# First block of a fused attention and MoE kernel: attention by pairs of units, an earlier bias, a constant added on GpSimd, and weights converted two tiles at a time

## The chip, the cores and the metric

The kernel runs on one core of a Trainium2 chip. The metric is the device time of one execution in microseconds. The profile is one execution of its own, whose trace has the start and length of each instruction. PE is TensorE, DVE is VectorE, ACT is ScalarE, POOL is GpSimd and SP is SyncE, which here only issues transfers (DMAs). L335 means line 335 of the kernel before.

## The reference

Attention for 4 batches, 8 heads, 576 positions and 64 channels, with a bias from a small network of the relative position, then two feed-forward stages on 2304 tokens of 512 channels:

```python
scores = scale * np.matmul(q, k.transpose(0, 1, 3, 2))
x = (psi_rel / psi_i)[..., None]
h = np.maximum(x @ w1 + b1, 0.0)
bias = h @ w2
scores = scores + bias.transpose(2, 0, 1)[None, :, :, :]
scores = scores - np.max(scores, axis=-1, keepdims=True)
attn = np.exp(scores)
attn = attn / (np.sum(attn, axis=-1, keepdims=True) + 1e-09)
x = np.matmul(attn, v)             # to 2304 tokens x 512
gate = 1.0 / (1.0 + np.exp(-(x @ w_gate)))
x = gate * (x @ w_val) @ w_out     # 512 -> 1536 -> 512
h = x @ w_in                       # 512 -> 2048
g = h * np.clip(h + 3.0, 0.0, 6.0) / 6.0
out = g @ moe2_w_out               # 2048 -> 512
```

## The kernel before

The queries are cut into five chunks (`QC`: four of 128, one of 64). A unit is one chunk, one pair of heads and one batch: 16 units in a chunk of 128 queries. For a unit TensorE makes the scores (`att_qk`, L335), VectorE subtracts them from the bias and takes the minimum (`att_min`, L350), ScalarE takes the exponential and the sum of each row (`att_exp`, L360), `att_norm` adds 1e-9 to the sums (L367), takes the reciprocal (L368) and scales (L373 on VectorE, or L371 on ScalarE in chunk 1). Then TensorE transposes nine blocks of 128 (`att_tr`, three at a time, L386), ScalarE copies each three out (L389), and TensorE multiplies with the values (`att_av`, L430); `att_x` writes the result as a high and a low half (L455, L456). Multiplies of full float32 are counted double in the trace (x20 for the ten of `att_av`), since each runs as two.

In the lead, only attention of chunk 0 runs, with the bias tables of the first chunks; its order on PE, ACT, DVE and SP is that of the code. Then come five blocks, one for each chunk. A block has 68 steps (`moe_steps`), and a step is 12 products of 128 by 512 (`product`, L613) of a chunk's tokens with one tile of weights; in the last block, with half the columns, steps are shorter and some have eight (L607). Block k also carries the attention of chunk k+1 and the bias of later chunks as events, each with a time in steps; an event is run in the code before the step at or after its time. In block 0 PE and SP keep the order of the code, and a scheduler orders ACT and DVE; in the later blocks only PE keeps it. From chunk 2 on, attention is by pairs of units (`pair_qk`, `pair_soft`, `pair_av`).

Weights come as packed 64-bit words (`wpack`). In block 0 each tile of 512 words is turned into a high and a low half (`w_split`: ACT L575, DVE L576, L577, L580, ACT L585, DVE L586) and stored to `wsp` in DRAM (`w_store`, L591). Later blocks load it from there (`w_load`, L535, 512 KB), `WA` steps ahead of its use. PSUM has two double banks for scores (`s_ps`) and four single banks (`mm_ps`).

## Time and profile before

| | us |
|---|---|
| median of 3 runs | 1105.45 |
| lowest and highest of them | 1104.69 and 1105.76 |
| the profiled execution | 1102.25 |
| its span | 1100.2 |
| TensorE busy in it | 1088.0 |
| VectorE busy in it | 679.8 |

The span is the time from the first to the last instruction in the trace; the execution's own time has some 2 us around it. All starts and windows below are counted from the start of the span. A row with "idle before" names in brackets how long the engine stood still before the instruction and what ended it.

### The profile page before, as it was taken

The page shows a single profiled execution, that of the slowest core. Times are in us where ns is not written, and L with a number is a line of the kernel's source. Part 1 is how long each engine was busy: PE and PEld are TensorE (multiplying, and loading weights), DVE is VectorE, ACT ScalarE, POOL GpSimd, SP SyncE. Part 2 cuts the span into 40 slices and gives each one's busy share as a digit, 9 for nine tenths or more (in the row PEclk, how much of TensorE's full clock was granted, in tenths as well). Part 3 has the DMA queues.
Part 4 walks back from the last instruction along what each step waited for, and adds up shares of the span by engine and source line. Part 5 has one row for each costly group of instructions (what it writes and reads, how often), then busy time and mean ns, then how long its engine had stood idle before and what let it go on. Part 6 is the DMA issues. An engine that isn't in the chain of part 4 may idle for free.

```text
span 1100.2 us, 19627 instructions
## 1 busy us (share of the span) xinstructions
PE 1088.0 (99%) x6964; PEld 873.7 (79%) x6964; DVE 679.8 (62%) x1571; ACT 534.7 (49%) x1087; POOL 129.9 (12%) x248
## 2 busy tenths in 40 slices
PE   8999999999999999999999999999999999999998
PEld 4777777777777787878778878788878888888898
DVE  8899998898972466887735654656352417153433
ACT  7887686798872534555424342444032214123332
...
GB/s 235 369 179 296 376 396 374 387 322 370 392 291 235 212 278 288 283 318 287 308 320 249 288 248 276 263 264 248 287 289 212 286 225 280 212 242 309 370 371 272
DMA packets 118768, 321.96 MB, mean 293 GB/s; under 512 B 21008, under 2 KB 29712, under 8 KB 118672
## 3 DMA queue, kind: packets, MB, share of 16 engines
...
q14 instruction: 40, 0.33, 0.1%
...
## 4 chain that ended last, share of the span: by engine, by line
PE 82%; DVE 7%; ACT 4%; DMA 3%; issue 2%; SPq 1%; DVEq 0%; ACTq 0%
PE ps L613 61%; PE ps L430 7%; PE ps L607 6%; PE ps L477 2%; PE ps L386 2%; PE ps L335 2%; PE ps L171 1%; DVE cm L577 1%; DMA kt<-kd 1%; DVE wp L586 1%; DVE cm L580 1%; PE ps L483 1%; ACT cm L575 1%; DVE s L350 1%; DMA wd<-wpack 1%
## 5 line engine op out<-in xcount | busy, mean ns | idle before, releaser
L613 PE MATMUL ps<-xyh,wp 128*128 128x512 f32 (+1 forms) x1472 | 431.2, 379 | 0.2
L613 PEld LDWEIGHTS ps<-xyh,wp 128*128 128x128 f32 x1472 | 263.3, 188 | 58.1 <-DVE m L499 2.7
L613 PE MATMUL ps<-gh,wp 128*128 128x512 f32 (+1 forms) x980 | 298.9, 385 | 0.4 <-ACT gh L628 0.4
L613 PE MATMUL ps<-xyl,wp 128*128 128x512 f32 x640 | 249.7, 390 | 0.3 <-DVE xyl L632 0.3
L613 PEld LDWEIGHTS ps<-gh,wp 128*128 128x128 f32 x980 | 178.7, 188 | 37.7 <-issue 2.5
L613 PE MATMUL ps<-gl,wp 128*128 128x512 f32 x448 | 174.8, 390 | 0.2 <-DVE gl L630 0.2
L409 POOL DMA_DIRECT2D pT<-t x192 | 94.4, 500 | 495.1 <-DMA wp<-wsp 205.1
L628 ACT ACTIVATE gh<-tmp 128x512 fp32r<-128x512 f32 (+1 forms) x140 | 82.1, 587 | 127.5 <-DVE tmp L651 85.1
L613 PEld LDWEIGHTS ps<-xyl,wp 128*128 128x128 f32 x640 | 120.2, 188 | 24.9 <-DVE xyl L632 0.8
L360 ACT ACTIVATE s<-s,m 128x576 f32<-128x576 f32 x144 | 110.4, 769 | 23.8 <-DVE m L499 17.9
L630 DVE TENSOR_TENSOR gl<-tmp,gh 128x512 fp32r<-128x512 f32 x112 | 76.5, 685 | 35.7 <-ACT gh L628 34.8
L613 PEld LDWEIGHTS ps<-gl,wp 128*128 128x128 f32 x448 | 84.2, 188 | 17.1 <-DVE gl L630 0.7
L430 PEld LDWEIGHTS ps<-pT,vt 128*64 128x64 f32 x1600 | 79.3, 137 | 17.0 <-issue 11.6
L430 PE MATMUL ps<-pT,vt 128*64 128x128 f32 (+1 forms) x1600 | 92.1, 266 | 0.5 <-ACT pT L389 0.4
L657 DVE SCALAR_TENSOR_TENSOR tmp<-tmp,ps 128x512 f32<-128x512 f32 (+1 forms) x80 | 50.0, 628 | 55.2 <-ACT tmp L656 53.6
L651 DVE SCALAR_TENSOR_TENSOR tmp<-tmp,ps 128x512 f32<-128x512 f32 x48 | 32.7, 682 | 74.5 <-PE ps L613 73.8
L656 ACT ACTIVATE tmp<-ps 128x512 f32<-128x512 f32 (+1 forms) x80 | 43.9, 548 | 44.3 <-PE ps L613 44.0
L455 ACT ACTIVATE xyh<-ps 128x128 fp32r<-128x128 f32 (+1 forms) x52 | 16.4, 316 | 98.7 <-PE ps L430 98.5
L681 POOL DMA_DIRECT2D outT<-acc x40 | 27.7, 740 | 269.0 <-DVE acc L672 250.3
L399 DVE STREAM_TRANSPOSE t<-s 128x1152 f32<-128x1152 f32 x40 | 54.3, 1369 | 0.4
L373 DVE TENSOR_SCALAR s<-s,r 128x576 f32<-128x576 f32 x112 | 53.2, 517 | 1.4
L456 DVE TENSOR_TENSOR xyl<-ps,xyh 128x128 fp32r<-128x128 f32 (+1 forms) x48 | 16.0, 333 | 58.9 <-ACT xyh L455 58.6
...
## 6 DMA issues: line engine op xcount, KB each, us to landing
wp<-wsp SPq DMA_DIRECT2D x272, 512.0 KB, 5.1
wd<-wpack SPq DMA_DIRECT2D x68, 512.0 KB, 6.4
wsp<-wp SPq DMA_DIRECT2D x68, 512.0 KB, 6.0
...
pT<-t SPq DMA_DIRECT2D x128, 72.0 KB, 4.5
...
```

Source lines behind the costliest of these rows:

```text
L360: nc.scalar.activation(out=s[:, h], in_=s[:, h], func=AF.Exp, scale=-1.0, bias=d["m"][:, h:h + 1], accum_out=r[:, h:h + 1],)
L373: nc.vector.tensor_scalar(out=s[:, h], in0=s[:, h], scalar1=r[:, h:h + 1], scalar2=None, op0=ALU.mult)
L399: nc.vector.transpose(out=tn_q[0][:, :, x], in_=st[u]["s"].rearrange("p h j -> p (h j)").rearrange("p (t q j) -> p q t j", q=4, j=32),)
L409: (nc.sync if p[0][0] < 4 and i > 1 else nc.gpsimd).dma_start(out=pt[32 * q:32 * q + 32, i].rearrange("j u t i -> j (u t i)"), in_=t[32 * ...
L430: nc.tensor.matmul(out=po[64 * h:64 * h + 64, n * a:n * a + n], lhsT=vt[:, v], rhs=pt[:, m * a:m * a + m, k, :], start=(t == 0), stop=(t = ...
L607: nc.tensor.matmul(out=o, lhsT=w[:, c, :], rhs=x, start=(first and c == 0 and w is wh), stop=(last and c == 3 and w is wh),)
L613: nc.tensor.matmul(out=ps[:, 0:nt], lhsT=w[:, c, :], rhs=x[:, 0:nt], start=(first and c == 0 and i == 0), stop=(last and c == 3 and i == 2),)
L628: nc.scalar.activation(out=hi, in_=src, func=AF.Copy, scale=scale)
L630: nc.vector.tensor_tensor(out=lo, in0=src, in1=hi.bitcast(F32), op=ALU.subtract)
L651: nc.vector.scalar_tensor_tensor(out=th, in0=th, scalar=1.0, in1=ps, op0=ALU.add, op1=ALU.mult)
L656: nc.scalar.activation(out=t, in_=ps, func=AF.Relu, bias=3.0)
L657: nc.vector.scalar_tensor_tensor(out=t, in0=t, scalar=6.0, in1=ps, op0=ALU.min, op1=ALU.mult)
```

## The change

Four things are changed.

1. Attention of chunk 1, which runs in block 0, goes by pairs of units. `pair_qk` makes the scores of two units in a row (for this chunk in full float32: first columns 320 to 575 into two single banks, then columns 0 to 319 into two double banks), `pair_soft` does the softmax of each, `att_trs` makes the nine transposes of a unit in a row into two double banks with two copies by ScalarE, and `pair_av` multiplies both units with their values. First scores stand before step 13 (16 in the order of before), the last values behind step 62 (at the block's end before). The bias of chunk 1 stands at steps from 1.0 on, 1.6 apart (2.0 and 2.0).
2. For chunks 0 and 1 the addition of 1e-9 to the sums is done by GpSimd instead of VectorE.
3. `w_split` converts two tiles at a time, every other step, except for tiles 2 and 3. Its scratch comes from the pools of transposed scores and of the bias. Packed tiles are loaded seven steps ahead.
4. Converted tiles lie in pairs (three pairs instead of six tiles), and the later blocks load four steps ahead instead of five; a pair's two loads are issued together when its space is free.

```diff
 SU = S + 31
-WA = 5
+WA = 4
+WR = 7
 WB = 3
...
     z_p = pool("z", 2)
-    w_p = pool("w", 6)
+    w_p = pool("w", 3)
 
...
         s, r = st[u]["s"], st[u]["r"]
-        nc.vector.tensor_scalar(out=r, in0=r, scalar1=1e-9, scalar2=None, op0=ALU.add)
+        q = nc.gpsimd if u[0] < 2 else nc.vector
+        q.tensor_scalar(out=r, in0=r, scalar1=1e-9, scalar2=None, op0=ALU.add)
         nc.vector.reciprocal(out=r, in_=r)
...
         )
+
+    def att_trs(u):
+
+        d = st[u]
+        pt = d["pt"] = A["pt"].tile([128, 9, NQ], F32, name="pT")
+        p = d["s"].rearrange("p h j -> p (h j)")
+        for k0, nb in ((0, 2), (6, 1)):
+            ps = s_ps()
+            for t in range(3 * nb):
+                nc.tensor.transpose(
+                    out=ps[:, t // 3, t % 3 * NQ:t % 3 * NQ + NQ], in_=p[:, 128 * (k0 + t):128 * (k0 + t) + 128],
+                    identity=id_t,
+                )
+            nc.scalar.activation(
+                out=pt[:, k0:k0 + 3 * nb].rearrange("p (a t) n -> p a (t n)", a=nb),
+                in_=ps[:, 0:nb, 0:3 * NQ], func=AF.Copy,
+            )
 
...
         c, hp, _ = p[0]
-        n = QC[c][1]
+        n, fast = QC[c][1], c in (2, 3)
         tails = [mm_ps(), mm_ps()]
...
                 b = u[2]
-                for i in range(3 if n == NQ else 1):
+                for i in range(3 if fast else 1):
                     for h in range(2):
...
                         o = tails[h][:, w * x:w * x + w] if j0 else st[u]["ps"][:, h, 0:NT]
-                        if n == NQ:
+                        if fast:
                             (qh, ql), (kh, kl) = q_q[c, hp], kv_q[u][0]
...
         att_norm(u)
+        if u[0] == 1:
+            return
         att_turn(p, x)
...
 
-    wq, wf_q = {}, {}
+    wq, wf_q, wp_q = {}, {}, {}
+
+    def w_tiles(n, k=1):
+
+        if n % 2 == 0:
+            wp_q[0] = w_p.tile([128, 2, 2, 512], F32R, name="wp")
+        for x in range(k):
+            wq[n + x] = wp_q[0][:, (n + x) % 2]
+        return wp_q[0][:, n % 2:n % 2 + k]
 
...
         if n < NSTEP:
-            wd = A["wf"].tile([128, 512, 2], U32, name="wd")
-            nc.sync.dma_start(out=wd.rearrange("p a b -> p (a b)"), in_=wpack[n].bitcast(U32))
-            wf_q[n] = wd
+            if n % 2 == 0:
+                wf_q[0] = A["wf"].tile([128, 2, 512, 2], U32, name="wd")
+            nc.sync.dma_start(
+                out=wf_q[0][:, n % 2].rearrange("p a b -> p (a b)"), in_=wpack[n].bitcast(U32)
+            )
+            wf_q[1, n] = wf_q[0][:, n % 2:2]
         else:
-            wp = w_p.tile([128, 2, 4, 128], F32R, name="wp")
-            nc.sync.dma_start(out=wp.rearrange("p s c m -> p s (c m)").bitcast(F32), in_=wsp[n % NSTEP])
-            wq[n] = wp
+            nc.sync.dma_start(out=w_tiles(n)[:, 0].bitcast(F32), in_=wsp[n % NSTEP])
 
...
             nc.sync.dma_start(out=wsp[n], in_=wv.bitcast(F32))
-            del wf_q[n], cm_q[n]
-
-    def w_split(n):
+            del cm_q[n]
+
+    def w_split(n, k=2):
 
...
             return
-        wd = wf_q.pop(n)
-        low, high = wd[:, :, 0], wd[:, :, 1]
-        m = A["cv"].tile([128, 512], U32, name="cm")
-        f = m.bitcast(F32)
+        wd = wf_q[1, n][:, 0:k]
+        low, high = wd[:, :, :, 0], wd[:, :, :, 1]
+        if n < 18:
+            m = A["pt"].tile([128, 9, NQ], F32, name="pT").rearrange("p t n -> p (t n)")
+        else:
+            m = z_p.tile([128, 4, S], F32, name="z").rearrange("p g j -> p (g j)")
+        f = m[:, 0:512 * k].rearrange("p (s a) -> p s a", s=k)
+        m = f.bitcast(U32)
         nc.scalar.activation(out=f, in_=high.bitcast(F32), func=AF.Copy, scale=2.0 ** -112)
...
         )
-        wp = w_p.tile([128, 2, 4, 128], F32R, name="wp")
-        wv = wp.rearrange("p s c m -> p s (c m)")
-        nc.scalar.activation(out=wv[:, 0], in_=f, func=AF.Copy)
-        nc.vector.tensor_tensor(out=wv[:, 1], in0=f, in1=wv[:, 0].bitcast(F32), op=ALU.subtract)
-        wq[n] = wp
+        wv = w_tiles(n, k)
+        nc.scalar.activation(out=wv[:, :, 0], in_=f, func=AF.Copy)
+        nc.vector.tensor_tensor(out=wv[:, :, 1], in0=f, in1=wv[:, :, 0].bitcast(F32), op=ALU.subtract)
 
...
         if 2 <= n < NSTEP:
-            nc.sync.dma_start(out=wsp[n], in_=wq[n].rearrange("p s c m -> p s (c m)").bitcast(F32))
+            nc.sync.dma_start(out=wsp[n], in_=wq[n].bitcast(F32))
 
...
         wp = wq.pop(n)
-        wh, wl = wp[:, 0], wp[:, 1]
+        wh, wl = (wp[:, s].rearrange("p (c m) -> p c m", c=4) for s in range(2))
         if first:
...
     with ExitStack() as lead:
-        for name, bufs in (("pt", 2), ("s", 3), ("k", 6), ("v", 7), ("bo", 3), ("wf", 2), ("cv", 2)):
+        for name, bufs in (("pt", 2), ("s", 3), ("k", 6), ("v", 7), ("bo", 3), ("wf", 1), ("cv", 2)):
             A[name] = lead.enter_context(tc.tile_pool(name=name + "l", bufs=bufs))
...
     conv = ExitStack()
-    for name, bufs in (("pt", 2), ("wf", 4), ("cv", 2)):
+    for name, bufs in (("pt", 2), ("wf", 3)):
         A[name] = conv.enter_context(tc.tile_pool(name=name + "c", bufs=bufs, reuse_waits="tile"))
...
     ctx.enter_context(tc.issue_after(gate_act.ins))
-    for n in range(2, WA + 1):
+    for n in range(2, WR):
         w_load(n)
...
 
-    def chunk_att(c, t0, t1, lag):
+    def chunk_att(c, t0, t1):
 
         us = units[c]
-        d = (t1 - t0) / (len(us) - 1 + lag)
+        ps = [tuple(us[i:i + 2]) for i in range(0, len(us), 2)]
+        d = (t1 - t0 - 6.2) / (len(ps) - 1)
         ev = [
-            (t0 - 2 * d, lambda: att_load(us[0], False)),
-            (t0 - d, lambda: (bias_read(us[0]), load_rows(us[1]), load_k(us[1]))),
+            (t0 - 6, lambda: (load_rows(us[0], False), load_k(us[0]), load_k(us[1]), load_v(us[0]))),
+            (t0 - 1.8, lambda: (bias_read(us[0]), load_v(us[1]))),
         ]
-        for i, u in enumerate(us):
+        for i, p in enumerate(ps):
             a = t0 + d * i
 
-            def first(u=u, nxt=us[i + 2] if i + 2 < len(us) else None):
-                if nxt:
-                    load_rows(nxt)
-                    load_k(nxt)
-                att_qk(u)
-                att_min(u)
-                att_exp(u)
-                att_norm(u)
-            if i:
-                ev.append((a + 0.5, lambda u=u: load_v(u)))
-            for part in range(3):
-                ev.append((a + lag * d - 3 + part, lambda u=u, p=part: att_tr(u, p, mm_ps)))
-            ev.append((a + lag * d - 0.01, lambda u=u: (att_av(u, mm_ps), att_x(u))))
+            def first(p=p, nxt=ps[i + 1] if i + 1 < len(ps) else ()):
+                for u in nxt:
+                    load_rows(u)
+                    load_k(u)
+                pair_qk(p)
+                pair_soft(p, 0)
+
             ev.append((a, first))
+            ev.append((a + 1.5, lambda p=p: pair_soft(p, 1)))
+            if i + 1 < len(ps):
+                ev.append((a + 0.5, lambda p=ps[i + 1]: [load_v(u) for u in p]))
+            for x, u in enumerate(p):
+                ev.append((a + 3.9 + 1.2 * x, lambda u=u: att_trs(u)))
+            ev.append((t1 if i + 1 == len(ps) else a + d - 0.01, lambda p=p: pair_av(p)))
         return ev
...
             ev.append((1.0, lambda: nc.sync.dma_start(out=td_t[:, t0:], in_=td[:, t0:])))
-            ev += chunk_bias(1, 2.0, 2.0, NG1 + 2)
-            ev += chunk_att(1, 15.5, last, 2)
+            ev += chunk_bias(1, 1.0, 1.6, NG1 + 2)
+            ev += chunk_att(1, 12.6, 62.2)
         elif k == 1:
...
             if k == 0:
-                if n + WA + 1 < NSTEP:
-                    w_load(n + WA + 1)
-                for x in range(WB - 1 if i == 0 else WB, WB + 1):
-                    w_store(n + x - 1)
-                    w_split(n + x)
+                if i == 0:
+                    w_split(2, 1)
+                    w_split(3, 1)
+                if n + WR < NSTEP:
+                    w_load(n + WR)
+                w_store(n + 1)
+                if i % 2:
+                    w_split(n + WB)
             if n + WA >= NSTEP:
...
             moe_step(k, i, P, mm_ps)

```

On POOL, from its start to the output of the first block (`biasD` are the bias tables in DRAM, `r` the sums of a unit), there stood:

```order
L977 MEMSET const-uint8-127 128x1
L983 UNCONDITIONAL_BRANCH
L261 DMA biasD_84<-bo 128x2x576 x4
L221 DMA biasD_85<-bo 16x8x607 x8
L681 DMA outT<-acc 256x1x128 x8
```

and now:

```order
L1013 MEMSET const-uint8-127 128x1
L1019 UNCONDITIONAL_BRANCH
L262 DMA biasD_84<-bo 128x2x576 x4
L222 DMA biasD_85<-bo 16x8x607 x4
L369 ISA
L369 TENSOR_SCALAR r<-r 128x2 x16
L222 DMA biasD_85<-bo 16x8x607 x4
L369 TENSOR_SCALAR r<-r 128x2 x16
L713 DMA outT<-acc 256x1x128 x8
```

The 32 additions are new, and so is the ISA row ahead of them, which stands behind the first four stores of the table of chunk 1.

On PE, in the middle of block 0, one unit of before (the order counts a float32 multiply once; between the rows with three transposes stand 12 products):

```order
L613 MATMUL ps<-gh,wp 128x512
L430 MATMUL ps<-pT,vt 64x128 x10
L335 MATMUL ps<-kt,qt 128x288 x4
L386 MATMUL ps<-id_t,s 128x128 x3
L613 MATMUL ps<-gh,wp 128x512
...
L613 MATMUL ps<-gh,wp 128x512
L386 MATMUL ps<-id_t,s 128x128 x3
L613 MATMUL ps<-gh,wp 128x512
```

and one pair of units now (48 products stand behind the scores, 12 between the two rows of transposes and 12 behind them):

```order
L645 MATMUL ps<-xyh,wp 128x512
L449 MATMUL ps<-pT,vt 64x128 x20
L502 MATMUL ps<-kt,qt 128x256 x4
L502 MATMUL ps<-kt,qt 128x320 x4
L645 MATMUL ps<-xyh,wp 128x512
...
L645 MATMUL ps<-xyh,wp 128x512
L404 MATMUL ps<-id_t,s 128x128 x9
L645 MATMUL ps<-xyh,wp 128x512
```

Values and scores of two units stand together, and the transposes are no longer cut into three.

On DVE, at the start of block 0, behind the conversion of tiles 2 and 3 (`cm` before and `pT` now are the scratch, `wd` packed and `wp` converted weights; the first conversion of before is that of tile 4, the second that of tile 5; L651 and L630 belong to the products):

```order
L586 TENSOR_TENSOR wp<-cm,wp 128x512 x2
L576 TENSOR_SCALAR cm<-cm 128x512
L577 SCALAR_TENSOR_TENSOR cm<-wd,cm 128x512
L576 TENSOR_SCALAR cm<-cm 128x512
L580 SCALAR_TENSOR_TENSOR cm<-wd,cm 128x512
L577 SCALAR_TENSOR_TENSOR cm<-wd,cm 128x512
L651 SCALAR_TENSOR_TENSOR tmp<-tmp,ps 128x512
L580 SCALAR_TENSOR_TENSOR cm<-wd,cm 128x512
L586 TENSOR_TENSOR wp<-cm,wp 128x512
L630 TENSOR_TENSOR gl<-tmp,gh 128x512
L586 TENSOR_TENSOR wp<-cm,wp 128x512
```

and now, with tiles 4 and 5 in the first 1024-wide conversion, tiles 6 and 7 in the second:

```order
L619 TENSOR_TENSOR wp<-pT,wp 128x512 x2
L610 TENSOR_SCALAR pT<-pT 128x1024
L611 SCALAR_TENSOR_TENSOR pT<-wd,pT 128x1024
L610 TENSOR_SCALAR pT<-pT 128x1024
L683 SCALAR_TENSOR_TENSOR tmp<-tmp,ps 128x512
L614 SCALAR_TENSOR_TENSOR pT<-wd,pT 128x1024
L611 SCALAR_TENSOR_TENSOR pT<-wd,pT 128x1024
L662 TENSOR_TENSOR gl<-tmp,gh 128x512
L614 SCALAR_TENSOR_TENSOR pT<-wd,pT 128x1024
L619 TENSOR_TENSOR wp<-pT,wp 128x2x512
```

The last row completes tiles 4 and 5 together; before, tile 4 was complete two rows ahead of tile 5.

## Rows read from the trace of the kernel before

**Rows 1.** The page: the span and the engines' busy time.

```profile
span 1100.2 us, 19627 instructions
...
PE 1088.0 (99%) x6964; PEld 873.7 (79%) x6964; DVE 679.8 (62%) x1571; ACT 534.7 (49%) x1087; POOL 129.9 (12%) x248
```

**Rows 2.** What PE waited for: total us, times, longest.

```profile
PE ps L179 <- ACT z L156: 1.2, 3, 0.9
```

**Rows 3.** Stretches: us busy (instructions) of engines, granted clock, DMA share, GB/s.

```profile
200.00:250.00 50.00, 50.00 (x322) 39.16 (x322) 46.92 (x100) 42.71 (x88) 0.00 (x0) 1.00 0.94 343
```

**Rows 4.** Timeline of PE in the lead: start, us, engine, line.

```profile
35.31 1.24 PE L335 MATMUL ps<-kt,qt 64*128 64x288 f32 x8 [0.95 <-DMA kt<-kd]
36.49 1.21 PE L386 MATMUL ps<-id_t,s 128*128 128x128 f32 x9
37.62 1.31 PE L430 MATMUL ps<-pT,vt 128*64 128x128 f32 x20
```

**Rows 5.** Timeline of POOL from the start.

```profile
0.25 0.10 POOL L977 MEMSET const-float32-0.0<- 128x1 f32 x1 [0.25 <-issue]
...
26.46 1.13 POOL L221 DMA_DIRECT2D biasD<-bo  x2 [2.45 <-DVE bo L199]
```

**Rows 6.** Timeline of DVE in the lead.

```profile
28.20 0.17 DVE L368 RECIPROCAL r<-r 128x2 f32<-128x2 f32 x1
```

**Rows 7.** Timeline of PE in block 0, one unit.

```profile
153.43 1.31 PE L430 MATMUL ps<-pT,vt 128*64 128x128 f32 x20
...
156.47 0.39 PE L613 MATMUL ps<-xyl,wp 128*128 128x512 f32 x1
...
158.53 0.39 PE L613 MATMUL ps<-xyl,wp 128*128 128x512 f32 x1
...
159.00 0.49 PE L386 MATMUL ps<-id_t,s 128*128 128x128 f32 x3
159.24 0.47 PE L613 MATMUL ps<-xyh,wp 128*128 128x512 f32 x1
159.56 0.40 PE L613 MATMUL ps<-xyl,wp 128*128 128x512 f32 x1
...
165.27 1.31 PE L430 MATMUL ps<-pT,vt 128*64 128x128 f32 x20
```

**Rows 8.** Timeline of PE in block 1: a pair's values, then a bias.

```profile
470.81 2.40 PE L430 MATMUL ps<-pT,vt 128*64 128x128 f32 x40
473.14 0.96 PE L171 MATMUL ps<-z,w2b_t 128*32 128x448 f32 x8
```

**Rows 9.** Timeline of PE in block 0, the unit with a wait.

```profile
295.43 0.87 PE L430 MATMUL ps<-pT,vt 128*64 128x128 f32 x10
296.68 0.87 PE L430 MATMUL ps<-pT,vt 128*64 128x128 f32 x10 [0.38 <-ACT pT L389]
297.48 1.24 PE L335 MATMUL ps<-kt,qt 64*128 64x288 f32 x8
```

**Rows 10.** Timeline of PE at the end of block 0.

```profile
330.98 0.87 PE L430 MATMUL ps<-pT,vt 128*64 128x128 f32 x10
331.78 0.50 PE L613 MATMUL ps<-xyh,wp 128*128 128x512 f32 x1
```

**Rows 11.** Timeline of DVE at the start of block 0.

```profile
86.34 1.28 DVE L580 SCALAR_TENSOR_TENSOR cm<-wd,cm 128x512 uint32<-128x512 uint32 x2
...
89.30 0.43 DVE L576 TENSOR_SCALAR cm<-cm 128x512 uint32<-128x512 uint32 x1
```

**Rows 12.** Timeline of PE at the start of step 4.

```profile
96.38 0.61 PE L613 MATMUL ps<-xyh,wp 128*128 128x512 f32 x2
```

**Rows 13.** Groups of ACT by shape in block 0: busy us, mean ns.

```profile
L360 ACT ACTIVATE s<-s,m 128x576 f32<-128x576 f32 x16 | 12.3, 771 | 2.0 <-DVE m L350 2.0
```

**Rows 14.** Transfer issues in block 4: KB each, median us to landing.

```profile
wp<-wsp SPq DMA_DIRECT2D x75, 512.0 KB, 5.2
```

**Rows 15.** Timeline of PE in block 4.

```profile
1009.81 3.92 PE L607 MATMUL ps<-xyh,wp 128*128 128x256 f32 x22
```

6 lines of the change are left out of this document (3 added, 3 removed).

## The prediction

> **What bounds the kernel now.** I read the page first: TensorE is busy for 1088.0 of the 1100.2 us [rows 1]. The list of what TensorE waits for comes next, because a nearly full engine can only gain where it still stands still: its longest entry is 1.2 us over three waits, all others are below that [rows 2]. So nothing in this change can win by feeding TensorE sooner, except at single places of less than 1 us. It can win by giving TensorE less to do, and lose by putting a wait on it. The table of stretches gives the reserve of the other engines in the first block: between 200 and 250 us VectorE works 46.92 of 50 us, ScalarE 42.71, and the 16 transfer engines are 94% busy [rows 3]. A wait placed on VectorE there, or a tile converted late, has little room. The granted clock is full in that row, so the clock gives nothing back.
>
> Two stretches then matter. In the lead (attention of the first 128 queries) TensorE's timeline is a row of scores, transposes and values, 1.18, 1.13 and about 1.2 us, with one wait of 0.95 us for a transfer of keys just before 35.31 [rows 4]; from there on it runs through. In the first block each unit (a head pair of one batch) is put between 36 products of 512 columns.
>
> **Attention by pairs.** The period of a unit runs from its values at 153.43 to the next at 165.27, 11.84 us [rows 7]. Products follow each other at (158.53 - 156.47)/9 = 0.229 us [rows 7], so 36 of them are 8.24 and a unit costs 3.60 us, two cost 7.20. Of the new pair, the 40 value multiplies in a row cost 473.14 - 470.81 = 2.33 [rows 8], as measured in the next block; two sets of scores 2 x (36.49 - 35.31) = 2.36 [rows 4] (256 and 320 columns instead of 2 x 288, the same columns); the first product behind a group takes 0.32 instead of 0.229 [rows 7], so 0.09. The nine transposes in a row have no row in a block: three of them between products cost 159.56 - 159.00 - 0.229 = 0.33 [rows 7], which gives 0.99 for nine, and nine in the lead take 1.13 before the next group [rows 4], with 0.09 for the first product 1.22. A pair is therefore 4.78 + 2 x (0.99 to 1.22) = 6.76 to 7.22, and saves 0.44 to nothing. I take the middle, 0.2, since nine in a row are as in the lead and products stand around them as in the block: 8 x 0.2 = **1.6 us gained** (0 to 3.5).
>
> Two single places go with the old order. At 295.43 the values of a unit are split by a wait for the copy of its transposes and last until 297.48, 2.05 us [rows 9] against 1.31 for such a group [rows 4]: **0.7** if no pair meets such a wait (0 otherwise). The last unit's values stand in two halves around the block's end, the first of 331.78 - 330.98 = 0.80 [rows 10]; two halves are 1.60 against 1.31: **0.3**.
>
> ScalarE's share of a pair is the same work: copies of 768 and 384 instead of three of 384, and the same exponentials and scalings. The earlier bias of the second chunk moves the same 32 multiplies one step ahead; TensorE has no wait there, so I cost it at nothing, covered by products.
>
> **The constant on GpSimd.** The add of 1e-9 to a unit's sums leaves VectorE (32 of them). It is worth about 0.2 us of VectorE per unit, as the reciprocal of the same size behind it takes 0.17 [rows 6], and TensorE doesn't wait for VectorE at these places, so the gain is nothing. The price is another. The order of GpSimd shows a new instruction of its own, the row that reads only ISA, ahead of the first add; by its name in the program it reloads the engine's code library. It stands behind the transfer issue that ends at 26.46 + 1.13 = 27.59 [rows 5], and the reciprocal behind it is wanted at 28.20 [rows 6]. VectorE's reciprocal waits for the add, behind it on VectorE the scaling, behind that TensorE's transposes. In this stretch VectorE's chain sets TensorE's pace, and the wait of 0.95 for keys at 35.31 [rows 4] is the reserve that I find behind it; from there TensorE's rows follow each other. So a reload that costs R delays the rest of the program by 27.59 + R + 0.2 - 28.20 - 0.95, that is by R - 1.4 if R is above 1.4, and by nothing below.
>
> No row of before has such an instruction. The nearest on its engine are the first memsets, 0.10 us each [rows 5]; if code has to be fetched, the nearest is a transfer, 5.2 us from issue to landing [rows 14]. The bounds are then 0 and 5.2 - 1.4 = 3.8 us. I take nothing, by the rows of the same engine, which runs these memsets within the first half microsecond of the program, before any code could have been fetched for them. This is a choice between two ends, not a middle, and the other end is a rival below.
>
> The Trainium skill, "GPSIMD Engine Reference", section on how an instruction is dispatched, speaks against my choice: the first call to freshly loaded kernel code pays about 6 us with no visible instruction. By that figure the delay would be an estimated 4.6 us instead of none. No row of before shows such a load.
>
> **Conversion over two tiles.** Each step used to convert one tile of 512 columns with four VectorE instructions and two of ScalarE; now every other step converts two at once, so fewer instructions with the same elements. VectorE's saving is hidden like the above. What it costs is that two tiles come ready together, the first of them later. The only place without reserve is the start. In the order of VectorE behind the two single tiles stand, up to the last instruction of tiles 4 and 5: two shifts, five 1024-wide two-input operations and two 512-wide ones of the products. A 512-wide shift took 0.43 us, a two-input one 1.28/2 = 0.64 [rows 11]; with double width at double price that is 2 x 0.86 + 5 x 1.28 + 2 x 0.64 = 9.4 us. Starting at 89.30 [rows 11] it ends at 98.7, while step 4 starts at 96.38 [rows 12] and asks for the low half in its third product, at about 96.9. That would be a wait of 1.8 us; fixed parts of an instruction are paid once for two tiles, and the first products need not be on time either, so the lower bound is 0. I take **0.5 lost**, nearer to 0, because back-to-back starts on VectorE are closer together than the durations in a row.
>
> **Loads in the later blocks.** Loads are issued in pairs, four steps ahead instead of five, for the even tile. In the last block 22 products of a stage take 3.92 us [rows 15], so a step of eight takes 1.43 and four steps 5.7 us, while a load lands in 5.2 (median) [rows 14]. Steps of the blocks before are nearly twice as long (12 x 0.229 = 2.7). The even tile asks for nothing that the odd one didn't have behind it in the same queue, so I cost it at nothing; above, it is bounded by a few loads that land late in the last block, 2 us.
>
> **Sum.** 1.6 + 0.7 + 0.3 - 0.5 = 2.1 us less. The profiled execution took 1102.25 us, its span 1100.2, so 1100.15 there; the runs' median is 1105.45, 3.2 above the profiled one, and with the same difference the forecast is **1103.3 us**.
>
> **Rivals.** (a) *The reload costs a transfer's time.* 3.8 us lost at 28 us less 2.1 gained: 1.7 slower, 1107.1. For it: an instruction that names a reload has bytes to bring, and TensorE's transposes there are chained to the reciprocal through VectorE. Against it: GpSimd needs nothing of the kind for its first instructions [rows 5]. It decides from R = 3.5 us on, where the loss equals the gain. By the Trainium skill's 6 us ("GPSIMD Engine Reference", the same section) it would come out at an estimated 1108.0.
>
> (b) *A pair's softmax is late.* Between a pair's scores and the first nine transposes stand four steps, 48 x 0.229 = 11.0 us. ScalarE alone needs 4 exponentials of 0.77 [rows 13] and up to 4 scalings of the same size, 6.2 us, and VectorE must first bring eight minima through a queue that now holds 1024-wide instructions of up to 1.28 us (twice the 0.64 above). If each pair waits 0.5 us, eight lose 4.0: 1107.3. Against it: the second unit's transposes stand 12 products behind the first's, and a similar pair form runs in the next blocks, while the longest entry among TensorE's waits is 1.2 us in all [rows 2].
>
> (c) *Nothing but the stalls changes*, nine transposes at the dear end: 0.7 + 0.3 - 0.5 = 0.5 faster, 1104.9; part of my own case.
>
> **Chances.** My case, with (c) as its upper part: 0.50, from 1100.9 (all terms at their good ends: 3.5 + 0.7 + 0.3 gained) to 1105.9 (no saving in the pairs, 1.5 at step 4), half of it more than 0.2% faster. Rival (a) 0.32, from 1105 to 1109. Rival (b) 0.18, from 1104 to 1109. A measurement of this kernel tells about 0.2% (2.2 us) from no change: faster means below 1103.2, slower above 1107.7. My case splits 0.25 and 0.25; (a) 0.02, 0.13 and 0.17; (b) 0.03, 0.04 and 0.11. Sums: faster 0.30, same 0.42, slower 0.28. The range that leaves out one in ten on each side is 1101.0 to 1108.6.
>
> **What would show it.** Right: TensorE's timeline passes the transposes at 36.49 [rows 4] at the same time, pairs in the first block cost about 7.0 us beyond their products, and no wait for a scaled tile. Wrong: a gap of TensorE of over 2 us between 28 and 36, with VectorE waiting for GpSimd's sum (rival a); waits of the new transposes for ScalarE's scaling (rival b); a wait of about 1 us at the fifth step; or waits for loaded tiles in the last block.

## The result, and the profile after

The changed kernel takes 1113.20 us in the median of 4 runs (1112.57 to 1115.27), the kernel before 1105.07 (1104.41 to 1105.76). The ratio is 1.0087, with a 95% interval of 1.0075 to 1.0100: slower by 8.1 us in the medians and by some 9.6 by the ratio, outside the range of 1101.0 to 1108.6 that was forecast. The profiled execution of the changed kernel took 1115.27 us, the highest of the four, at a mean granted clock of 0.993 over its span; in the other three it was 0.995 to 0.997.

The page has TensorE as busy as before [rows 1], and 13 us more of span (8 in the medians). The row of the granted clock has a slice below 9, which the kernel before doesn't have:

```profile
span 1113.5 us, 19187 instructions
...
PE 1089.2 (98%) x6964; PEld 880.2 (79%) x6964; DVE 669.8 (60%) x1467; ACT 522.6 (47%) x999; POOL 141.6 (13%) x280
...
PEclk9999999999989999999999999999999999999999
```

The stretch from 100 to 333 us, most of block 0, of the changed kernel (busy us and instructions of PE, PEld, DVE, ACT and POOL, then granted clock, share of the transfer engines, GB/s), and below it of the kernel before:

```profile
100.00:333.00 233.00, 223.75 (x1316) 179.73 (x1315) 196.19 (x342) 169.62 (x274) 11.99 (x22) 0.97 0.93 344
```

```profile
100.00:333.00 233.00, 232.54 (x1365) 181.10 (x1358) 204.68 (x426) 181.08 (x357) 6.31 (x10) 1.00 0.97 361
```

TensorE stood still for 233.00 - 223.75 = 9.25 us instead of 0.46, and its mean granted clock is 0.97. VectorE, ScalarE and the transfer engines all do less per microsecond than before, so over the whole stretch none of them is busier than the kernel before had it. Measured from the first product of block 0 to the first of block 1 (product 817 in the trace), the block takes 261.6 us instead of 251.8; the lead is 0.3 us shorter, and blocks 1 to 4 together are 3.8 longer.

What TensorE waited for from 80 to 333 us, the four longest entries (us in total, times, longest):

```profile
PE ps L645 <- DVE wp L619: 2.3, 2, 1.8
PE ps L645 <- ACT gh L660: 2.0, 1, 2.0
PE ps L404 <- ACT pT L408: 2.0, 1, 2.0
PE ps L645 <- DVE gl L662: 1.8, 1, 1.8
```

Converted weights (`wp`, L619), the copies of transposes (`pT`, L408), and the high and low halves of a step's result (`gh`, `gl`, L660 and L662): four kinds of work of ScalarE and VectorE, each late once or twice, the longest of each by some 2 us. Before, the list had only one of these, 0.4 us for a copy. The wait of the transposes (L404) for a copy is one for space: the nine transposes of a pair's second unit need the double banks that the copies of the first unit's transposes (L408) empty.

**GpSimd's addition** is the first thing that was in doubt. GpSimd's timeline in the lead, and VectorE's first reciprocal:

```profile
26.30 1.12 POOL L222 DMA_DIRECT2D biasD<-bo  x2 [2.44 <-DVE bo L200]
27.63 0.21 POOL L369 TENSOR_SCALAR r<-r 128x2 f32<-128x2 f32 x1 [0.21 <-ACT s L361]
```

```profile
27.88 0.17 DVE L370 RECIPROCAL r<-r 128x2 f32<-128x2 f32 x1
```

The first addition starts 0.21 us behind the last transfer issue, a time put down to ScalarE's sum that it needs, and takes 0.21. The reload ahead of it shows no time. The reciprocal stands at 27.88 instead of 28.20 [rows 6], and TensorE's transposes of [rows 4] at 36.15 instead of 36.49:

```profile
34.98 1.24 PE L336 MATMUL ps<-kt,qt 64*128 64x288 f32 x8 [0.93 <-DMA kt<-kd]
36.15 1.20 PE L388 MATMUL ps<-id_t,s 128*128 128x128 f32 x9
```

**A pair** has this shape in the timeline of TensorE: values at 173.51, scores at 175.85 and 177.99 the first product, then nine transposes in a row at 189.01:

```profile
173.51 2.40 PE L449 MATMUL ps<-pT,vt 128*64 128x128 f32 x40
175.85 2.21 PE L502 MATMUL ps<-kt,qt 64*128 64x256 f32 x16
177.99 0.50 PE L645 MATMUL ps<-gh,wp 128*128 128x512 f32 x1
178.32 0.39 PE L645 MATMUL ps<-gl,wp 128*128 128x512 f32 x1
...
189.01 1.15 PE L404 MATMUL ps<-id_t,s 128*128 128x128 f32 x9
189.91 0.48 PE L645 MATMUL ps<-gh,wp 128*128 128x512 f32 x1
190.22 0.39 PE L645 MATMUL ps<-gl,wp 128*128 128x512 f32 x1
```

From the values to the second product are 178.32 - 173.51 - 0.229 = 4.58 us, and nine transposes cost 190.22 - 189.01 - 0.229 = 0.98. A pair is 4.58 + 2 x 0.98 = 6.5 us, with the product ahead of it, 0.08 longer than 0.229, some 6.6, against 7.20 for two units [rows 7]: 0.6 saved, some 4.5 us in eight pairs.

**A wait** is dearer than it looks. TensorE at the end of the block:

```profile
316.76 0.39 PE L645 MATMUL ps<-gh,wp 128*128 128x512 f32 x1
319.15 0.50 PE L645 MATMUL ps<-gh,wp 128*128 128x512 f32 x1 [2.01 <-ACT gh L660]
321.47 0.80 PE L645 MATMUL ps<-gl,wp 128*128 128x512 f32 x1 [1.81 <-DVE gl L662]
322.07 1.05 PE L645 MATMUL ps<-gh,wp 128*128 128x512 f32 x2
322.92 0.63 PE L645 MATMUL ps<-gl,wp 128*128 128x512 f32 x1
...
326.55 0.84 PE L645 MATMUL ps<-gh,wp 128*128 128x512 f32 x2
327.22 0.40 PE L645 MATMUL ps<-gl,wp 128*128 128x512 f32 x1
```

```profile
322.07:326.55 4.48, 4.48 (x17) 3.80 (x16) 4.48 (x10) 4.25 (x7) 1.34 (x2) 0.50 0.27 102
```

Two waits of 2.01 and 1.81 us stand behind each other, and then products start 0.43 apart ((322.92 - 322.07) / 2) instead of 0.229, up to 326.55. The granted clock of that stretch is 0.50 (second row): TensorE is at the lower of its two levels, 1.2 GHz instead of 2.4. A mean granted clock of 0.97 over 233 us is 7 us of full clock not granted (part of it while TensorE stood still), where before had none. Not every wait is followed by such a stretch: in pairs_only (below) TensorE stood still for 6.4 us, at most 1.55 at a time, and in single_converted once for 1.77, both at a mean clock of 1.00 from 100 to 333 us. ScalarE just ahead of the wait of 2.01 us shows the cause there, with VectorE's row for its operand in front:

```profile
314.57 0.69 DVE L689 SCALAR_TENSOR_TENSOR tmp<-tmp,ps 128x512 f32<-128x512 f32 x1 [0.51 <-ACT tmp L688]
```

```profile
314.95 1.14 ACT L609 ACTIVATE z<-wd 128x1024 f32<-128x1024 f32 x1
315.98 0.59 ACT L688 ACTIVATE tmp<-ps 128x512 f32<-128x512 f32 x1
316.46 1.06 ACT L618 ACTIVATE wp<-z 128x1024 fp32r<-128x1024 f32 x1
317.40 1.18 ACT L408 ACTIVATE pT<-ps 128x768 f32<-128x768 f32 x2
318.46 1.16 ACT L660 ACTIVATE gh<-tmp 128x512 fp32r<-128x512 f32 x2
```

TensorE wants the high half (L660). Its operand (`tmp`, L689) is complete at 315.26, yet it stands at 318.46, behind a scaled copy of two packed tiles (L609, 1.14 us), a high half of two converted tiles (L618, 1.06) and the copies of transposes (L408, 1.18). Long instructions ahead of it in ScalarE's queue held back the short one that was waited for.

### The profile page after: what moved, and what is told of

It is laid out like the page before. It is cut to its first block, busy times and chain, and to the rows that moved or that the text cites. A ratio compares the mean times of both kernels' runs of the same rounds, so it can differ in the third digit from the quotient of the medians.

```text
span 1113.5 us, 19187 instructions
## 1 busy us (share of the span) xinstructions
PE 1089.2 (98%) x6964; PEld 880.2 (79%) x6964; DVE 669.8 (60%) x1467; ACT 522.6 (47%) x999; POOL 141.6 (13%) x280
## 4 chain that ended last, share of the span: by engine, by line
PE 76%; DVE 8%; DMA 7%; ACT 5%; issue 2%; SPq 1%; POOL 0%; DVEq 0%; ACTq 0%
PE ps L645 56%; PE ps L449 6%; PE ps L639 5%; PE ps L496 2%; DMA wp<-wsp 2%; DMA wd<-wpack 2%; DMA kt<-kd 2%; DVE wp L619 1%; PE ps L388 1%; DVE s L518 1%; PE ps L336 1%; ACT s L361 1%; PE ps L502 1%; PE ps L172 1%; ACT s L373 1%
## 5 line engine op out<-in xcount | busy, mean ns | idle before, releaser
L645 PE MATMUL ps<-gh,wp 128*128 128x512 f32 (+1 forms) x980 | 295.9, 384 | 2.9 <-ACT gh L660 2.9
L660 ACT ACTIVATE gh<-tmp 128x512 fp32r<-128x512 f32 (+1 forms) x140 | 82.0, 587 | 132.1 <-DVE tmp L683 86.9
L662 DVE TENSOR_TENSOR gl<-tmp,gh 128x512 fp32r<-128x512 f32 x112 | 76.4, 686 | 36.1 <-ACT gh L660 35.4
L449 PE MATMUL ps<-pT,vt 128*64 128x128 f32 (+1 forms) x1600 | 89.1, 265 | 1.5 <-DMA wp<-wsp 1.4
L689 DVE SCALAR_TENSOR_TENSOR tmp<-tmp,ps 128x512 f32<-128x512 f32 (+1 forms) x80 | 49.9, 628 | 53.2 <-ACT tmp L688 51.8
L474 ACT ACTIVATE xyh<-ps 128x256 fp32r<-128x256 f32 (+1 forms) x44 | 15.1, 344 | 97.7 <-PE ps L449 97.7
L679 ACT ACTIVATE tmp<-ps 128x512 f32<-128x512 f32 x48 | 28.5, 593 | 60.2 <-PE ps L645 60.2
L518 DVE CUSTOM_DVE_ANT_0 s<-ps,bm,m 128x320 f32<-128x320 f32 x112 | 56.2, 545 | 0.0
```

The source lines that it names most:

```text
L449: nc.tensor.matmul(out=po[64 * h:64 * h + 64, n * a:n * a + n], lhsT=vt[:, v], rhs=pt[:, m * a:m * a + m, k, :], start=(t == 0), stop=(t = ...
L518: nc.vector.tensor_tensor_reduce(out=d["s"][:, h, j0:j1], in0=x, in1=bm_q[c, hp][:, h, j0:j1], scale=-(D ** -0.5), scalar=top, op0=ALU.add ...
L645: nc.tensor.matmul(out=ps[:, 0:nt], lhsT=w[:, c, :], rhs=x[:, 0:nt], start=(first and c == 0 and i == 0), stop=(last and c == 3 and i == 2),)
L660: nc.scalar.activation(out=hi, in_=src, func=AF.Copy, scale=scale)
L662: nc.vector.tensor_tensor(out=lo, in0=src, in1=hi.bitcast(F32), op=ALU.subtract)
L689: nc.vector.scalar_tensor_tensor(out=t, in0=t, scalar=6.0, in1=ps, op0=ALU.min, op1=ALU.mult)
```

## The experiments

The list of waits gave the first theory, T: conversion by two tiles makes the waits, as converted tiles and what stands behind 1024-wide instructions come late, while pairs only save. Rival S put them down to the pairs, whose softmax comes in bursts and late; rival C to both together.

The experiments were timed beside runs of the kernel before with medians of 1103.3 to 1103.5 us; the changed kernel's ratio is that of the first result. The table gives for each kernel the ratio to it, the length of block 0 (start of the 817th product less start of the first, from the trace of one profiled execution), and how long TensorE stood still from 100 to 333 us (233 less its busy time there). The last two columns come from one execution each, so a difference of 1 us in them says little by itself (executions of the kernel before differ by 3).

| kernel | ratio, 95% interval | block 0, us | TensorE idle, us |
|---|---|---|---|
| before | | 251.8 | 0.5 |
| changed | 1.0087, 1.0075 to 1.0100 | 261.6 | 9.3 |
| pairs_only | 1.0024, 1.0015 to 1.0034 | 254.5 | 6.4 |
| two_tiles_only | 1.0071, 1.0054 to 1.0087 | 259.9 | 5.1 |
| add_on_vector | 1.0117, 1.0090 to 1.0143 | 260.8 | 10.6 |
| five_ahead | 1.0102, 1.0087 to 1.0117 | 261.6 | 10.0 |
| before_half_loads | 1.0005, 0.9996 to 1.0014 | 253.0 | 1.6 |
| pairs_half_loads | 1.0075, 1.0057 to 1.0093 | 262.8 | 9.1 |
| after_half_loads | 1.0155, 1.0140 to 1.0170 | 267.4 | 13.5 |
| pairs_late | 1.0037, 1.0026 to 1.0048 | 255.7 | 6.6 |
| pairs_light | 0.9964, 0.9950 to 0.9977 | 247.9 | 2.1 |
| after_light | 1.0001, 0.9992 to 1.0011 | 252.1 | 4.3 |
| before_light | 0.9977, 0.9967 to 0.9987 | 249.7 | 0.0 |
| pairs_slack | 1.0029, 1.0017 to 1.0041 | 256.4 | 7.2 |
| single_in_pairs | 1.0072, 1.0045 to 1.0099 | 257.9 | 4.6 |
| single_packed | 1.0047, 1.0032 to 1.0062 | 256.4 | 4.7 |
| single_converted | 1.0022, 1.0013 to 1.0032 | 254.3 | 3.2 |
| pairs_sub_pool | 1.0241, 1.0221 to 1.0261 | 277.9 | 18.7 |
| before_short | 1.0027, 1.0016 to 1.0038 | 250.6 | 0.0 |
| pairs_short | 1.0093, 1.0066 to 1.0119 | 253.0 | 5.2 |

### Which part of the change

**pairs_only**, the kernel before with the pairs (`chunk_att`, `att_trs` and the lines of `pair_qk` and `pair_soft` as in the change, not repeated here) and the earlier bias:

```diff
-            ev += chunk_bias(1, 2.0, 2.0, NG1 + 2)
-            ev += chunk_att(1, 15.5, last, 2)
+            ev += chunk_bias(1, 1.0, 1.6, NG1 + 2)
+            ev += chunk_att(1, 12.6, 62.2)
```

> The kernel before with attention of chunk 1 by pairs and the earlier bias alone: conversion by single tiles, loads five ahead and the constant on VectorE stay. Theory T (the conversion by two tiles with three pair buffers makes the waits of block 0; the pairs themselves are cheaper): no wait of TensorE above 0.5 us between 100 and 330 us, pairs at 6.7 us beyond their products, 1100 to 1102.5 us. Rival S (a pair's softmax bunches work on ScalarE and VectorE and its chain is late): waits of over 1 us in block 0 as in the changed kernel, 1107 or more. Rival C (only both together run short): like T here.

**two_tiles_only**, the changed kernel with those lines, `chunk_att` and `att_norm` as they were:

> The changed kernel with attention of chunk 1 by units and the bias times of before, and the constant on VectorE: conversion by two tiles, three pair buffers and loads four ahead stay. Theory T: waits of TensorE for converted tiles or evictions in block 0, 1109 to 1116 us. Rival S: no such waits, 1104 to 1107 (only the later blocks' waits for loads, about 1 to 2 us). Rival C (only both together run short): 1104 to 1107.

**add_on_vector**:

```diff
-        q = nc.gpsimd if u[0] < 2 else nc.vector
-        q.tensor_scalar(out=r, in0=r, scalar1=1e-9, scalar2=None, op0=ALU.add)
+        nc.vector.tensor_scalar(out=r, in0=r, scalar1=1e-9, scalar2=None, op0=ALU.add)
```

> The changed kernel with the addition of the constant back on VectorE. Theory T and rivals S and C: the same as the changed kernel, 1111.5 to 1115 us, since GpSimd's additions took 0.21 us and no gap stood ahead of the first. Rival G (VectorE's wait for GpSimd, 1.2 us at most in block 0, disturbs the order there): 1 to 4 us faster than the changed kernel.

**five_ahead**:

```diff
-WA = 4
+WA = 5
```

> The changed kernel with loads of the later blocks five steps ahead again, still in three pair buffers. If the shorter lead makes the later blocks' waits for loads (1.4, 0.8 and 0.2 us in the changed kernel's trace, with what follows them): 1.5 to 3 us faster than the changed kernel. If the pair buffers make them (a load can only start when both tiles of a pair are used up): the same as the changed kernel, within 1 us.

Both halves lose, and nearly add up: the pairs 0.24%, conversion by two tiles 0.71%, together 0.87% (1.17% in add_on_vector, where the addition is on VectorE as in the two halves). So theory T held for the conversion alone, and C fell. For the pairs S held in kind, with waits of over 1 us, but 1106.0 us lies between what T and S had said. The pairs save on TensorE and still make the block 2.7 us longer. In pairs_only TensorE waits, among others, for the scalings and copies of their own softmax (waits of TensorE in pairs_only):

```profile
PE ps L402 <- ACT s L371: 2.8, 2, 1.5
PE ps L402 <- ACT pT L406: 1.4, 2, 0.7
```

The addition on VectorE gave nothing back, rather the opposite, so no cost of GpSimd's part shows. Loads five ahead made blocks 1 to 4 shorter by 2.3 us in the profile (766.0 against 768.3 to the end of the span), but the timed ratio shows no gain. In two_tiles_only, with loads four ahead as well, these blocks took 765.0, only 0.5 more than before. So what the lead of the loads costs stays open.

### Transfers

The first block keeps the transfer engines 97% busy in the kernel before (the row above). Theory D held them to be the limit. From tile 5 on, packed words of every other tile (in the changed kernel of every other pair) aren't loaded, and the tile ahead of it is converted again, so the output is another one:

```diff
-        if n < NSTEP:
+        if 4 <= n < NSTEP and n % 2:
+            wf_q[n] = wf_q[n - 1]
+        elif n < NSTEP:
```

> The kernel before, but from tile 5 on every odd tile in block 0 is converted from the packed words of the even tile ahead of it, whose load serves both (wrong weights, the same instructions, 32 loads of 512 KB less of the first block's traffic of 87.6 MB). Theory D (block 0 runs at the limit of the transfer engines, so in the kernel before the loads arrive just in time and TensorE doesn't wait): no change, within 2 us of the kernel before. If the transfers held the kernel before too: 2 us faster or more.

> Attention by pairs and the earlier bias alone, with the same 32 loads left out (wrong weights, the same instructions). Theory D: the waits of TensorE in block 0 (7 us in the run of pairs alone) go for the most part, what the pairs save on TensorE is seen: 3 to 5 us faster than pairs alone, and 1 to 3 us faster than the kernel before. Rival O (the waits come from the order of ScalarE's and VectorE's queues, not from data): within 1.5 us of pairs alone.

> The changed kernel, but from tile 4 on every other pair of tiles in block 0 is converted from the packed words of the pair ahead (wrong weights, the same instructions, 32 loads of 512 KB less). Theory D: the waits in block 0 and the drops of the clock behind them go, 1100 to 1105 us. Rival O (the 1024-wide instructions in the queues of ScalarE and VectorE make the waits whatever the data do): 1110 us or more. Both in part: between.

**pairs_late** starts the pairs and the bias as late as the units had them:

```diff
-            ev += chunk_bias(1, 1.0, 1.6, NG1 + 2)
-            ev += chunk_att(1, 12.6, 62.2)
+            ev += chunk_bias(1, 2.0, 2.0, NG1 + 2)
+            ev += chunk_att(1, 15.5, 66.0)
```

> Attention by pairs alone, with the bias of chunk 1 at its old times (steps 2.0 on, 2.0 apart) and the pairs started at step 15.5 as the units were, ending at 66. Theory D (the early bias and the early loads of chunk 1 put more traffic into the stretch from 100 to 130 us, where the packed words then come late): the first waits (0.35, 1.55 and 0.53 us between 120 and 150 us, and the late products there) go, 2 to 4 us faster than pairs alone, 1101 to 1104 us on the scale of 1103.5 for the kernel before. Rival O: the same as pairs alone, within 1.5 us.

Theory D, as it was put, fell. With a fifth of the traffic gone the pairs got 6 us slower, and the changed kernel 7; no theory had said that. The stretch from 100 to 333 us of pairs_half_loads:

```profile
100.00:333.00 233.00, 223.87 (x1307) 180.93 (x1306) 205.50 (x475) 176.90 (x329) 3.55 (x6) 0.96 0.78 276
```

The transfer engines are at 0.78, and TensorE is idle for 9.1 us. Since the scheduler orders ScalarE and VectorE anew for each kernel, this run has another order there than pairs_only; it shows that the waits come without full transfer engines, not that the loads are free. Packed words still came late in it, later than in pairs_only (longest wait 2.72 us). ScalarE waited 6.40 us for them, and SyncE, whose transfers keep the order of the code, had stood 4.5 us before a load of values (L305) that waited for TensorE, ahead of the load of these words (L552, issued at 228.84; the second row is from SyncE's waits from 205 to 240 us):

```profile
235.25 0.67 ACT L596 ACTIVATE cm<-wd 128x512 f32<-128x512 f32 x1 [6.40 <-DMA wd<-wpack]
```

```profile
SPq L305 <- PE ps L447: 5.2, 2, 4.5
```

So the order of SyncE's transfers is a rival that no run tests. The later start gained nothing either.

### VectorE's time

Of the bit instructions of a conversion, one (L577 of before, which joins the lowest three bits of each weight) is left out, so weights are rounded down in these bits:

```diff
-        nc.vector.scalar_tensor_tensor(
-            out=m, in0=low, scalar=29, in1=m, op0=ALU.logical_shift_right, op1=ALU.bitwise_or
-        )
```

> Attention by pairs alone, with one VectorE instruction per converted tile in block 0 left out (the OR of the lowest three bits of each weight, about 0.6 us of VectorE per step of 2.73 us). Theory U (VectorE and ScalarE have too little time left in block 0, so a pair's burst of minima, exponentials and scalings makes converted tiles and evictions late): the waits in block 0 shrink to under 2 us of 7, 1100 to 1102.5 us. Rival L (a pair's own chain from scores to transposes is too long for its four steps, whatever else the engines do): less than 1.5 us faster than pairs alone.

> The changed kernel with the same VectorE instruction left out per two tiles (about 1.15 us of VectorE in 5.5). Theory U: 5 us or more faster than the changed kernel, 1107 or less. Rival B (three buffers of two tiles, and stores that have to land before a buffer is free, make the waits): within 2 us of the changed kernel.

> The kernel before with the same VectorE instruction of the conversion left out (the lowest three bits of each weight). Theory U (VectorE's time runs short with pairs, and not before, where TensorE hardly waits): within 1 us of the kernel before. If the instruction's time is paid in every kernel: 4 us or more faster.

**pairs_slack** gives a pair's chain one step more:

```diff
-                ev.append((a + 3.9 + 1.2 * x, lambda u=u: att_trs(u)))
+                ev.append((a + 4.9 + 1.1 * x, lambda u=u: att_trs(u)))
```

> Attention by pairs alone, with the transposes of each pair one step later (at 4.9 and 6.0 steps behind the scores instead of 3.9 and 5.1). Rival L: the waits for scalings ahead of the transposes (2.8 us, and 1.4 us for copies) go, 3 us or more faster than pairs alone. Theory U: those waits move to others (evictions, converted tiles), less than 1.5 us faster.

One step more changed nothing in the time, and TensorE's waits for scalings gave way to others (2.1 and 1.4 us for converted tiles, 1.7 for copies): rival L fell. One instruction less per tile changed much. The stretch from 100 to 333 us of pairs_only and of pairs_light:

```profile
100.00:333.00 233.00, 226.60 (x1347) 181.09 (x1346) 209.86 (x483) 179.50 (x336) 5.03 (x8) 1.00 0.96 353
```

```profile
100.00:333.00 233.00, 230.91 (x1374) 187.01 (x1374) 176.93 (x420) 176.62 (x333) 6.31 (x11) 1.00 0.97 366
```

VectorE goes from 209.86 us of 233 (90%) to 176.93 (76%), and TensorE's idle time from 6.4 to 2.1. The pairs are then level with before_light or slightly ahead (0.13%, with overlapping intervals; 247.9 against 249.7 us in block 0) instead of 0.24% behind before. The kernel before gains too, 0.23%, more than theory U had said, though its TensorE hardly waited there. So part of the pairs' 4.5 us is there when VectorE has room. VectorE's share alone doesn't decide, though: in the same stretch it was 88% in the kernel before and 89% in before_short (below), where TensorE stood still for 0.5 and 0.0 us. That bursts of minima, exponentials and scalings make something late is the reading that fits; it isn't shown apart from the new order that each edit brings.

The changed kernel gained most, from 1.0087 to 1.0001, where rival B had allowed 2 us. So what its buffers cost (next section) depends on VectorE's room as well.

### The two-tile conversion

**single_in_pairs** converts each tile by itself, with all buffers as in two_tiles_only:

```diff
-                if i % 2:
-                    w_split(n + WB)
+                if n + WB > 3:
+                    w_split(n + WB, 1)
```

> The kernel with two-tile conversion alone, but each tile converted by itself, one per step, in the same three pair buffers, with the same scratch, the same loads seven steps ahead and four steps ahead in the later blocks. If the 1024-wide instructions (a queue is held twice as long, both tiles are only ready together) make the loss: 1103 to 1106 us, no waits for converted tiles in block 0. Rival B (the buffers and their stores): 1108 us or more, with such waits.

**single_packed** then gives packed tiles six buffers of their own, **single_converted** instead the converted ones (the lines that take the tiles alone; first one kernel's, then the other's):

```diff
-                wf_q[0] = A["wf"].tile([128, 2, 512, 2], U32, name="wd")
+            wd = A["wf"].tile([128, 1, 512, 2], U32, name="wd")
...
-            wp_q[0] = w_p.tile([128, 2, 2, 512], F32R, name="wp")
+        t = w_p.tile([128, 1, 2, 512], F32R, name="wp")
```

> Single tiles converted one per step with three pair buffers for converted tiles as in the run of single tiles in pairs, but with six single buffers for packed tiles, so that a load waits for one conversion only. If the packed pairs made the loss (loads can start only after both tiles are converted): 1103 to 1106 us, no wait over 1 us between 130 and 150 us. If the converted pairs and their stores did: 1108 or more.

> The same with packed tiles still in three pair buffers, and six single buffers for converted tiles, so that a conversion waits for one tile's products and store only. If the converted pairs made the loss: 1103 to 1106 us. If the packed pairs did: 1108 or more, with late packed tiles between 115 and 140 us.

I had held the 1024-wide instructions to be the cost. No such cost shows: single tiles in pair buffers are as slow (1.0072 against 1.0071, each to within 0.2 to 0.3%). Buffers by single tiles give back 0.50% for the converted ones, clear of noise, and 0.25% for the packed ones, where the intervals overlap; at 1108.1 single_packed also met what was expected if the converted pairs made the loss, and single_converted, at 1106.2, nearly did. So most of the loss is in the pairs of buffers for converted tiles: three pairs hold as much as six tiles, but a half that is used up can't be filled before the other half is used up and stored as well. The 0.22% that single_converted still loses isn't divided further: packed pairs, loads seven and four ahead, and the shared scratch are left in it, and no run had both kinds of buffers single. In single_in_pairs the longest wait is at one place: ScalarE waits for packed tiles, and 10 us later TensorE waits 2.37 us for a converted one (the mean granted clock from 130 to 150 us is 0.91).

```profile
129.79 0.67 ACT L608 ACTIVATE z<-wd 128x512 f32<-128x512 f32 x1 [1.66 <-DMA wd<-wpack]
...
132.28 0.68 ACT L608 ACTIVATE z<-wd 128x512 f32<-128x512 f32 x1 [0.26 <-DMA wd<-wpack]
```

```profile
141.00 0.73 PE L644 MATMUL ps<-xyh,wp 128*128 128x512 f32 x2 [2.37 <-DVE wp L618]
```

### Two attempts at a faster version

**pairs_sub_pool** has the last instruction of a conversion on GpSimd:

```diff
-        nc.vector.tensor_tensor(out=wv[:, 1], in0=f, in1=wv[:, 0].bitcast(F32), op=ALU.subtract)
+        nc.gpsimd.tensor_tensor(out=wv[:, 1], in0=f, in1=wv[:, 0].bitcast(F32), op=ALU.subtract)
```

> Attention by pairs alone, with the last instruction of each conversion in block 0 (the subtraction that makes the low half, 0.6 us of VectorE per step) on GpSimd, nothing left out. Theory U: if GpSimd takes no more than some 2 us for one, the waits in block 0 shrink as with the instruction left out, 1099 to 1103 us, faster than the kernel before. If GpSimd takes over 2.7 us for one, it becomes the bound of the conversion: 1120 us or more.

**before_short** and **pairs_short** join lowest bits and sign first, in a scratch `e`, so that only one VectorE instruction stands between ScalarE's two:

```diff
+        nc.vector.tensor_scalar(out=e, in0=low, scalar1=29, scalar2=None, op0=ALU.logical_shift_right)
+        nc.vector.scalar_tensor_tensor(
+            out=e, in0=high, scalar=0x80000000, in1=e, op0=ALU.bitwise_and, op1=ALU.bitwise_or
+        )
+        nc.vector.scalar_tensor_tensor(
+            out=m, in0=m, scalar=3, in1=e, op0=ALU.logical_shift_left, op1=ALU.bitwise_or
+        )
```

> The kernel before with the conversion's three bit instructions in another order, the same result: the lowest bits and the sign are joined first, in a scratch of their own, without ScalarE's scaled copy, and only the third instruction needs that copy. VectorE's time is the same, the chain behind ScalarE is one instruction instead of three (1.2 us shorter). If the chain's length makes the waits: 1 to 3 us faster than the kernel before. If VectorE's time does: within 1 us of it.

> Attention by pairs alone with the same shorter chain. If the chain's length makes the pairs' waits: 3 us or more faster than pairs alone (2.5 above the kernel before), and as fast as the kernel before or faster. If VectorE's time does (theory U): within 1.5 us of pairs alone.

GpSimd takes 1.37 us for one subtraction, within what was expected, and the kernel still lost 2.4%. Groups of VectorE by shape from 150 to 250 us, in pairs_only and in pairs_sub_pool, and GpSimd's in the latter (busy us, mean ns):

```profile
L599 DVE SCALAR_TENSOR_TENSOR cm<-wd,cm 128x512 uint32<-128x512 uint32 x28 | 19.2, 687 | 0.3
L596 DVE SCALAR_TENSOR_TENSOR cm<-wd,cm 128x512 uint32<-128x512 uint32 x27 | 18.6, 688 | 0.4
```

```profile
L599 DVE SCALAR_TENSOR_TENSOR cm<-wd,cm 128x512 uint32<-128x512 uint32 x25 | 23.0, 918 | 0.5
L596 DVE SCALAR_TENSOR_TENSOR cm<-wd,cm 128x512 uint32<-128x512 uint32 x25 | 22.7, 909 | 0.6
```

```profile
L605 POOL TENSOR_TENSOR wp<-cm,wp 128x512 fp32r<-128x512 f32 x25 | 34.3, 1373 | 66.4 <-ACT wp L604 57.2 <-PE ps L500 4.5 <-DMA wsp<-wp 2.6
```

VectorE's two-input bit instructions went from 0.69 to 0.91 us in the mean. This mean hides two kinds, as rows of both engines show:

```profile
198.75 1.29 POOL L605 TENSOR_TENSOR wp<-cm,wp 128x512 fp32r<-128x512 f32 x1 [1.36 <-ACT wp L604]
```

```profile
198.90 1.69 DVE L596 SCALAR_TENSOR_TENSOR cm<-wd,cm 128x512 uint32<-128x512 uint32 x1
200.62 0.69 DVE L599 SCALAR_TENSOR_TENSOR cm<-wd,cm 128x512 uint32<-128x512 uint32 x1
```

The instruction that starts under GpSimd's subtraction (198.75 to 200.04) takes 1.69 us, ending 0.55 behind it; the next, with GpSimd idle, takes its usual 0.69. Of VectorE's 57 rows of L599 from 100 to 333 us, the 38 without such overlap take 0.69 in the mean. So VectorE lost back part of the time that it had given away. VectorE's share of the stretch is 84% here, below that of pairs_only, and TensorE's waits are the most of all (from 80 to 360 us 5.4 for copies, 4.2 for scalings, 3.2 for GpSimd's tiles): theory U's answer failed, and what makes the whole loss isn't shown.

The shorter chain made block 0 a little shorter (250.6 against 251.8, and 253.0 against 254.5 with pairs), so the chain may have a part, of 1 to 1.5 us in one execution each. Timed, both were slower than either answer had said (1106.64 and 1110.83 us, the latter with executions from 1108.16 to 1119.13, of which the lowest was profiled). In the profiles the loss came in the lead, which grew from 83.9 to 89.8 us (88.9 with pairs). VectorE's timeline there, in before_short:

```profile
72.77 0.43 DVE L577 TENSOR_SCALAR ce<-wd 128x512 uint32<-128x512 uint32 x1 [3.10 <-DMA wd<-wpack]
```

The first instruction no longer depends on ScalarE, so the scheduler put one for a tile of block 0 into the lead's queue, where it waited 3.10 us for its load, with the softmax of the lead behind it. Held back to block 0, before_short would be a candidate; this wasn't tried. No version without work left out beat the kernel before.

## Why the prediction was wrong

- *GpSimd's constant at nothing*: right, and so was the choice between the two ends. The first addition ran at 27.63, and TensorE passed the lead 0.3 us sooner. The rule of the Trainium skill ("GPSIMD Engine Reference", section on instruction dispatch), some 6 us for a first call, would have put it at an estimated 33; no run here shows such a time.
- *Pairs, 1.6 us gained*: right in direction, and too small. The work of eight pairs measured some 4.5 less, since nine transposes in a row cost 0.98, the cheap end of 0.99 to 1.22, and values and scores 4.66 instead of 4.78.
- *The two single places, 1.0*: both went, but the new order made others: 2.01 and 1.81 us at the block's end, 2.0 ahead of a pair's transposes.
- *Conversion over two tiles, 0.5 lost at step 4*: the step that failed. The place that it priced was no loss: VectorE completed tiles 4 and 5 at 97.81, and the bias multiplies, moved ahead of step 4 by the change, held its first product back to 97.88 (timelines of the changed kernel):

```profile
96.13 0.39 PE L645 MATMUL ps<-xyh,wp 128*128 128x512 f32 x1
96.45 1.50 PE L172 MATMUL ps<-z,w2b_t 128*32 128x384 f32 x16
97.88 0.50 PE L645 MATMUL ps<-xyh,wp 128*128 128x512 f32 x1
```

```profile
96.59 1.22 DVE L619 TENSOR_TENSOR wp<-pT,wp 128x1024 fp32r<-128x1024 f32 x1
```

  That this place cost nothing was luck of the order: in two_tiles_only, where the bias stands later, the wait is there, 0.82 us ahead of the third product of step 4, near the 0.5 that was taken:

```profile
99.08 0.73 PE L644 MATMUL ps<-xyh,wp 128*128 128x512 f32 x2 [0.82 <-DVE wp L618]
```

  I had looked for the cost in the width of the instructions and at the start, and had left the pair buffers uncosted. With the loads' new turn and the shared scratch they are what is left of the two-tile conversion in single_in_pairs, 0.72%, or some 8 us; single buffers for converted tiles alone bring it down to 0.22%.
- *The rest of a pair's work at nothing, and rival (b) at 0.18*: the second failure. TensorE's waits of 6.4 us in pairs_only, 5.9 more than before, ate the 4.5. Rival (b) named late softmax, and scalings are on the list of pairs_only; but one step more of slack didn't help, so it isn't that chain's length. pairs_light points to VectorE's room, with work in bursts; the cause stays open as far as each run also had a new order.
- *Each wait priced at its length*: behind waits of about 2 us products ran at half speed, 7 us of clock lost in block 0 of the profiled execution. The sum had no term for that.
- *Loads four ahead at nothing*: waits of 0.8 and 0.2 us for loaded tiles appeared in the later blocks, and one of 1.4 ahead of values, which the list puts down to such a load though values read no weights. They are 2.4 us together, and blocks 1 to 4 took 3.8 more, above the bound of 2; but two_tiles_only, with the same lead, took only 0.5 more, so the lead isn't shown to be the cause.
- *Reading of [rows 2]*: "single places of less than 1 us" overlooked one wait of 1.1 us near the start (L111); nothing hangs on it.

What stays open: how much of the pairs' waits is VectorE's time itself, and how much the order that the scheduler makes of it. Each edit changed that order, and before_half_loads (no gain) beside pairs_half_loads (6 us lost) shows that one edit, with the order that it brings, can be worth nothing in one kernel and several microseconds in another.
